# Two-layer pipeline on one Trainium2 core: the planner's order is refined in forward and backward passes, and one-lane loads are paced at 360 GB/s

## The chip, the cores and the metric

The kernel runs on one core of a Trainium2 chip. The metric is the device time in microseconds of one execution, the median of several runs. One further execution was taken with the hardware profiler; every row, wait and clock below comes from that one.

## What is computed

The input is a sequence of 2048 tokens of width 640. Block A is attention with a recurrent memory: the sequence is cut into 64 segments of 32 tokens, and each segment attends, with 32 heads of 192, to itself and to 8 memory rows. The memory rows of a segment's result are the memory of the next segment, so the segments of one layer can only run one after the other. Block B is a token mixer and an MLP with two layer norms and two gelus. Layers A, B, A, B follow each other.

```python
for s in range(n_seg):
    xs = x[:, s * seg_len:(s + 1) * seg_len, :].copy()
    h = jnp.concatenate([mem, xs], axis=1)
    q = jnp.einsum('btd,dhe->bhte', h, Wq)
    ...
    o = jnp.einsum('bhqk,bhke->bhqe', p, v)
    o = jnp.einsum('bhte,hed->btd', o, Wo)
    mem = o[:, :M, :].copy()
    outs.append(o[:, M:, :])
...
x = x + _A_ref(_layernorm(x, axis=-1), ...)
x = x + _B_ref(_layernorm(x, axis=-1), ...)
x = x + _A_ref(_layernorm(x, axis=-1), ...)
x = x + _B_ref(_layernorm(x, axis=-1), ...)
```

## The kernel before, in words

**Steps and lanes.** The kernel runs 69 steps. In step t, lane 0 computes segment t of the first attention layer and lane 1 segment t - 5 of the second, side by side, so that each weight is read once for both. Steps 0 to 4 have only lane 0 and steps 64 to 68 only lane 1; these ten are called one-lane steps here, and steps 5 to 63 two-lane steps. Block B runs in chunks of 64 tokens of each lane, one chunk in every two steps, in between the attention's work.

**Inside a step.** The heads are taken in four pairs of groups. For each pair come the key and query projections (`psk` and `psq`, line 612, functions `fn`), the value projection (`psv`, line 665 with two lanes, 700 with one, `fv`), and for each group of four heads a chain that goes from engine to engine: scores `pss` on TensorE (line 720, `fs`), the row extreme on VectorE (732), the exponential on ScalarE (739), the normalization on VectorE (743 to 745), transposes `pst` on TensorE (754, `f4`), their copy `PT` on ScalarE (762), attention times values `pso` on TensorE (771, `f6`), and its two half copies `oT` (782 on ScalarE, 784 on VectorE). The output projection `psy` (806, `f8`) reads `oT`. At the end of a step the memory rows are copied out of `psy` into the next step's input `hT` (833, `fm`); no projection of the next step can start ahead of that. In block B the pieces of w3 are line 1224 (`psh`), those of w4 line 1269 (`y`), and the gelu's steps lie between lines 894 and 907.

**Weights.** Part of the attention weights stays in SBUF. The rest is streamed by the SP queue into a ring of 12 slots of 384 KB (`RING_A`, tile `wst`, line 490): 23 loads in a step, since the last pair of a step is kept and used first in the next one. Block B's weights go through a ring of three (`wstB`, lines 526 to 532).

**What sets the order.** Nothing is issued where it stands in the source. Every operation is an `Op` with an engine, an estimated duration, a due time written by hand (a place within a step of nominally 48 units) and its dependences. `Plan.place` is a list scheduler on the host: it keeps a time for each engine, for each PSUM and ring slot and for one model of the DMA queues, and of the operations that could start about first on an engine it takes the one with the earliest due time. The resulting list is then emitted; each engine works through its own part of it in that order, and waits where a semaphore says so. The planner's times do not exist on the chip, with one exception: a load that the planner held back for the DMA queues (`paced`) gets a dependence on the last TensorE operation that had ended in the plan when the load was to start. So the load's moment on the chip is a place in TensorE's work. The rate that the planner grants to loads is `DMA_START` in step 0, `RATE_ONE` in the other one-lane steps and `DMA_RATE` in two-lane steps; only step 0's loads are never held back.

```python
s = max(s, srv - ahead(o))
o.paced = s > s0 + 1e-9
...
srv = max(s + DMA_FIRST, srv) + o.dma / (DMA_START if o.due < STEP else RATE_ONE if alone(o) else DMA_RATE)
done = srv + DMA_LAST + o.margin
```

Of the kernel before, what the change touches and what calls it, by code (L numbers as in the profile page):

```python
# [45 lines left out]
ONE = 56  # L46
WARM = (2, 4, 2, 1, 1, 1, 1, 6, 1, 1, 2, 1, 1)
SWITCH = 0.095
LAT = 0.12
PE_LAT = 0.3  # L50
DMA_RATE = 350.0e3
DMA_ISSUE = 0.37
DMA_FIRST = 0.8
DMA_LAST = 3.2
# [2 lines left out]
LEAD_B = 0.0  # L57
DMA_AHEAD = 1.0
DMA_AHEAD_ONE = 1.0
DMA_START = 385.0e3  # L60
RATE_ONE = 400.0e3
NSTEPS = 64
LAST_PACE = 0.55

# [25 lines left out]

class Op:
    __slots__ = ("e", "d", "due", "fn", "n", "succ", "ready", "slots", "start", "end", "dma", "i", "margin",
                 "paced", "last", "after", "mode")


class Plan:
# [8 lines left out]
    def add(self, e, d, due, fn, r=(), w=(), a=(), dma=0, queue=None, margin=0.0, after=(), mode=0, order=()):  # L105
        op = Op()
        op.mode = mode
        op.e, op.d, op.due, op.fn, op.dma, op.margin = e, d, due, fn, dma, margin
        op.succ, op.ready, op.n = [], 0.0, 0
        op.i = len(self.ops)  # L110
        op.paced = False
        op.last = None
        op.after = after
        preds = {*after, *order}
        slots = []
        for b in r:
            preds.update(b.writers)
        for b in w:
            preds.update(b.writers)
            preds.update(b.readers)  # L120
        for b in a:
            preds.update(b.base)
            preds.update(b.readers)
        for b in r:
            b.readers.append(op)
        for b in w:
            b.base = [op]
            b.writers = [op]
            b.readers = []
        for b in a:  # L130
            b.writers.append(op)
        for b in {id(b): b for b in (*r, *w, *a)}.values():
            if isinstance(b, Slotted):
                b.left += 1
                slots.append(b)
        op.slots = slots
        preds.discard(op)
        for p in preds:
            p.succ.append(op)
            op.n += 1  # L140
        self.ops.append(op)
        if queue is not None:
            self.queues.setdefault(queue, []).append(op)
        return op

    def place(self):
        in_queue = {}
        head = {}
        for q, lst in self.queues.items():
            lst.sort(key=lambda o: (o.due, o.i))  # L150
            for k, o in enumerate(lst):
                in_queue[o.i] = (q, k)
            head[q] = 0
        engines = sorted({o.e for o in self.ops})
        cand = {e: [] for e in engines}
        free = dict.fromkeys(engines, 0.0)
        waiting = {}

        def offer(o):
# [12 lines left out]
        mode = 0  # L172
        out = []

        def est(o, t):
            s = max(t, o.ready)
            need = {}
            for b in o.slots:
                if b.slot is None:
                    k, n = need.get(b.cls, (0, 0))  # L180
                    need[b.cls] = max(k, b.keep), n + 1
            for c, (k, n) in need.items():
                fs = self.free_slots[c]
                if len(fs) < n + k:
                    return None
                s = max(s, fs[n - 1][0])
            if o.e == "SP":
                s0 = s
                s = max(s, srv - ahead(o))
                o.paced = s > s0 + 1e-9  # L190
            return s

        def ahead(o):
            if o.due < STEP:
                return 1.0e9
            return DMA_AHEAD_ONE if alone(o) else DMA_AHEAD

        def alone(o):
            return o.due < LAG * STEP or o.due >= NSTEPS * STEP

        while left:
            best = None
            for e in engines:
                t = free[e]
                lst = cand[e]
                if not lst:
                    continue
                vals = []
                m = None
                for o in lst:  # L210
                    s = est(o, t)
                    if s is not None:
                        vals.append((s, o))
                        if m is None or s < m:
                            m = s
                if m is None:
                    continue
                if best is not None and m >= best[0]:
                    continue
                lim = m + (0.12 if e == "PE" else 0.05)  # L220
                stay = e == "PE" and mode
                s, o = min((so for so in vals if so[0] <= lim),
                           key=lambda so: (so[1].mode != mode if stay else False, so[1].due, so[1].i))
                if best is None or s < best[0]:
                    best = (s, o)
            assert best is not None, "no operation can be placed"
            s, o = best
            e = o.e
            for b in o.slots:
                if b.slot is None:  # L230
                    b.slot = self.free_slots[b.cls].pop(0)[1]
# [12 lines left out]
            left -= 1  # L244
            for b in o.slots:
                b.left -= 1
                b.free_at = max(b.free_at, done + LAT)
                if b.left == 0:
                    heapq.heappush(self.free_slots[b.cls], (b.free_at, b.slot))
                    self.free_slots[b.cls].sort()  # L250
            for x in o.succ:
                if o.dma:
                    at = done
                elif x.e == e:
                    at = o.end
                else:
                    at = o.end + (PE_LAT if e == "PE" else LAT)
                if at > x.ready:
                    x.ready = at
                x.n -= 1  # L260
                if x.n == 0:
                    offer(x)
            if o.i in in_queue:
                q, k = in_queue[o.i]
                head[q] = k + 1
                lst = self.queues[q]
                if k + 1 < len(lst) and lst[k + 1].i in waiting:
                    x = waiting.pop(lst[k + 1].i)
                    cand[x.e].append(x)
        return out  # L270
# [3 lines left out]
def kernel(  # L274
# [228 lines left out]
    def load_b(nm, a, e, due, c0=0, c1=None, last=False):  # L503
# [19 lines left out]
        def fn(op):  # L523
# [906 lines left out]
```

## Time and profile before

| what | value |
|---|---|
| median of 3 runs | 3384.89 us (3380.54 to 3385.96) |
| the profiled execution | 3382.05 us, its span 3380.3 us |
| TensorE busy in the span | 3191.1 us, 94% |
| VectorE, ScalarE busy | 2318.0 us, 1908.7 us |
| DMA | 860.40 MB, mean 255 GB/s |
| steps 1 to 4 (one lane), by the trace | 176.0 us, TensorE busy 151.36 us |
| steps 5 to 63 (two lanes) | 2861.7 us, TensorE busy 2775.39 us |
| steps 64 to 67 (one lane) | 184.6 us, TensorE busy 156.53 us |

The steps are cut at the 68 starts of ScalarE's copy of line 833, which ends a step's recurrence: 89.2, 265.2, 3126.9 and 3311.5 us are those after steps 0, 4, 63 and 67. In a row of waits the columns are the instruction, what it waited for, and then the total, the number and the longest. A release called "issue" is idle time for which the profile shows no semaphore.

### The profile page before, as it was taken

How to read it: one execution, taken by the hardware profiler on the slowest of the kernel's cores; microseconds unless marked ns; L12 is line 12 of the kernel's file. 1: busy time of each engine (PE TensorE's matmuls, PEld its weight loads, DVE VectorE, ACT ScalarE, POOL GpSimd, SP SyncE). 2: the span in 40 equal slices, each digit the busy share in tenths (PEclk: the TensorE clock that was granted, in tenths of full speed). 3: DMA queues.
4: the chain of work that ended last, by engine and by line, in shares of the span. 5: the costliest groups of instructions: out<-in, count | busy, mean ns of one | idle time of the engine just before them, and what ended most of it. 6: DMA issues, size and time to landing. Idle time of an engine off the chain costs nothing.

```text
span 3380.3 us, 173603 instructions
## 1 busy us (share of the span) xinstructions
PE 3191.1 (94%) x77341; PEld 2808.9 (83%) x77341; DVE 2318.0 (69%) x6857; ACT 1908.7 (56%) x4837; POOL 237.2 (7%) x485
## 2 busy tenths in 40 slices
PE   6889999999999999999999999999999999999887
PEld 4778888888888888888888888888888888888775
DVE  2665676777677777776767777677777777677665
ACT  2335565656555656565556656555666565556443
POOL 0000000000000000000000000000000000000000
PEclk7999999999999999999999999999999999999999
DMA  9776777778777876787778767877776778777875
GB/s 372 262 271 233 238 270 249 237 240 278 255 244 242 276 250 236 238 277 254 245 233 286 238 231 249 270 250 239 258 268 236 241 260 278 242 240 255 286 249 204
DMA packets 419559, 860.40 MB, mean 255 GB/s; under 512 B 40784, under 2 KB 208415, under 8 KB 418808
## 3 DMA queue, kind: packets, MB, share of 16 engines
q1 hardware_dynamic: 411512, 836.21, 72.2%
q8 instruction: 605, 9.91, 1.2%
q0 software_dynamic: 7136, 13.00, 1.2%
q14 instruction: 146, 1.20, 0.1%
q10 hardware_dynamic: 160, 0.08, 0.0%
HBM read 843.88 MB, written 5.24 MB: 251 GB/s over the span
## 4 chain that ended last, share of the span: by engine, by line
PE 81%; DVE 9%; DMA 4%; ACT 3%; issue 3%; SPq 1%; POOL 0%; DVEq 0%; ACTq 0%
PE psy L806 16%; PE psq L612 16%; PE psk L612 15%; PE psv L665 12%; PE pso L771 4%; PE pss L720 4%; PE y L1269 3%; PE pst L754 3%; PE psh L1224 3%; PE psv L700 2%; DVE oT L784 2%; PE hs L1161 1%; PE psh L1102 1%; ACT oT L782 1%; DMA wstB<-in_B_w_dram 1%
## 5 line engine op out<-in xcount | busy, mean ns | idle before, releaser
L612 PEld LDWEIGHTS <-wst 128*128 128x128 bf16 x19872 | 793.3, 99 | 21.9 <-issue 12.0
L806 PE MATMUL psy<-oT,wo 128*128 128x80 bf16 (+1 forms) x16560 | 685.2, 200 | 69.2 <-DVE oT L784 41.5
L645 ACT CAST V<-psv 96x384 bf16<-96x384 f32 (+3 forms) x1264 | 599.6, 474 | 212.9 <-PE psv L665 123.8
L806 PEld LDWEIGHTS <-wo 128*128 128x128 bf16 x16560 | 628.6, 99 | 81.9 <-issue 71.3
L732 DVE CUSTOM_DVE_ANT_1 pss<-pss,mask 80x320 f32<-80x320 f32 (+2 forms) x552 | 258.9, 469 | 333.9 <-PE pss L720 320.9
L612 PE MATMUL psq<-hT,wst 128*128 128x80 bf16 (+1 forms) x9936 | 474.2, 200 | 11.6 <-issue 7.8
L612 PE MATMUL psk<-hT,wst 128*128 128x80 bf16 (+1 forms) x9936 | 460.1, 200 | 1.5 <-issue 1.0
L665 PEld LDWEIGHTS <-hT 128*32 128x32 bf16 (+1 forms) x11840 | 295.6, 96 | 162.7 <-issue 11.5
L620 ACT CAST qT<-psq 128x480 bf16<-128x480 f32 (+1 forms) x552 | 290.9, 527 | 228.6 <-PE psq L612 224.8
L665 PE MATMUL psv<-wst,hT 128*32 128x384 bf16 x6512 | 367.2, 326 | 1.3 <-DMA wst<-in_A_Wv_dram 0.7
L784 DVE CAST oT<-pso 128x240 bf16<-128x240 f32 (+1 forms) x552 | 214.1, 388 | 224.4 <-ACT oT L782 195.1
L762 ACT COPY PT<-pst 80x320 bf16<-80x320 bf16 (+2 forms) x552 | 222.4, 403 | 214.8 <-PE pst L754 210.5
L612 PE MATMUL psk<-hT,wk 128*128 128x80 bf16 (+1 forms) x6624 | 320.6, 200 | 17.0 <-DVE hT L833 14.9
L612 PE MATMUL psq<-hT,wq 128*128 128x80 bf16 (+1 forms) x6624 | 321.7, 200 | 8.7 <-DMA wq<-in_A_Wq_dram 4.4
L635 ACT CAST kT<-psk 64x160 bf16<-64x160 f32 (+1 forms) x552 | 152.7, 277 | 303.9 <-PE pss L720 171.3
L665 PE MATMUL psv<-wv,hT 128*32 128x384 bf16 x5328 | 321.8, 328 | 0.0
L628 DVE CAST kT<-psk 128x320 bf16<-128x320 f32 (+1 forms) x552 | 255.2, 462 | 92.7 <-ACT kT L635 87.8
L612 PEld LDWEIGHTS <-wk 128*128 128x128 bf16 x6624 | 274.9, 99 | 26.4 <-issue 21.6
L782 ACT CAST oT<-pso 128x240 bf16<-128x240 f32 (+1 forms) x552 | 190.1, 344 | 175.0 <-PE pso L771 137.7
L612 PEld LDWEIGHTS <-wq 128*128 128x128 bf16 x6624 | 267.3, 100 | 10.3 <-issue 5.2
L771 PE MATMUL pso<-PT,V 80*128 80x80 bf16 (+2 forms) x4416 | 244.8, 197 | 23.7 <-ACT PT L762 13.8
L720 PE MATMUL pss<-kT,qT 128*128 128x80 bf16 (+2 forms) x3312 | 243.2, 210 | 9.6 <-issue 4.9
(148 smaller groups left out, 4238.2 us busy)
## 6 DMA issues: line engine op xcount, KB each, us to landing
wst<-in_A_Wk_dram SPq DMA_DIRECT2D x556, 384.0 KB, 5.3
wst<-in_A_Wq_dram SPq DMA_DIRECT2D x556, 384.0 KB, 5.4
wst<-in_A_Wv_dram SPq DMA_DIRECT2D x487, 384.0 KB, 5.4
wstB<-in_B_w_dram SPq DMA_DIRECT2D x495, 320.0 KB, 5.0
wstB<-in_B_w_dram SPq DMA_DIRECT2D x132, 160.0 KB, 4.4
wo<-in_A_Wo_dram SPq DMA_DIRECT2D x8, 960.0 KB, 12.3
xw<-in_A_x_dram POOLq DMA_DIRECT2D x31, 80.0 KB, 4.9
x2d<-vbg POOLq DMA_DIRECT2D x31, 80.0 KB, 5.2
```

What stands on the lines that cost most here:

```text
L612: nc.tensor.matmul(out=o[:, cc, 0:W], lhsT=wv(kc, GW * j + cc * P, GW * j + (cc + 1) * P), rhs=h[:, kc, cw:cw + W], start=(kc == 0 and cc ...
L620: nc.scalar.copy(out=qT[:, :, c0:c0 + N], in_=T(pq)[:, :, off:off + N])
L628: nc.vector.tensor_copy(out=k4[:, :, 0::3, c0:c0 + N], in_=p4[:, :, 0::2, off:off + N])
L645: (nc.vector.tensor_copy if e == "DVE" else nc.scalar.copy)(out=v_part(*dst), in_=a_)
L665: nc.tensor.matmul(out=o[32 * u:32 * u + n3, :], lhsT=left[:, kc, 32 * g3:32 * g3 + n3], rhs=wv(kc, a, a + GWH), start=(kc == 0), stop=(kc ...
L720: nc.tensor.matmul(out=o[0:m_, i * N:(i + w_) * N].rearrange("p (a b) -> p a b", a=w_), lhsT=qTw[:, c * NS:c * NS + m_], rhs=k_[:, j:j + w ...
L732: nc.vector.tensor_tensor_reduce(out=o, in0=o, in1=maskt.unsqueeze(1).to_broadcast([NR, HG, N]), scale=-scale, scalar=3.0e38, op0=ALU.add, ...
L762: nc.scalar.copy(out=Pt[0:KV, :, 0:N], in_=T(pst)[0:KV, :, c0:c0 + N])
L771: nc.tensor.matmul(out=o[:, 3 * hf + c, 0:N], lhsT=V_[0:KV, VP * hf + col:VP * hf + col + P], rhs=Pt[0:KV, 2 * hf + i2, 0:N], start=st, st ...
L782: nc.scalar.copy(out=o_[:, 3:6, off:off + N], in_=T(pso)[:, 3:6, 0:N])
L784: nc.vector.tensor_copy(out=o_[:, 0:3, off:off + N], in_=T(pso)[:, 0:3, 0:N])
L806: nc.tensor.matmul(out=o[:, m, cw:cw + W], lhsT=wo[:, cc, m * P:(m + 1) * P], rhs=o_[:, cc, 0:W], start=st, stop=True, skip_group_check=True)
```

## The change

`place` no longer schedules once. It schedules forward with the due times as priorities, then goes backward through that schedule and gives each operation the latest time at which it may start without moving the end, takes these times as the priorities of the next forward pass, and repeats that five times. The pass whose modelled end is the earliest is then made again and used. The order within the two SP queues still follows the due times. Apart from that two rates of the planner change: loads in step 0 from 385 to 375 GB/s and loads in the other one-lane steps from 400 to 360 GB/s. The operations themselves, their instructions and their data are the same 20,726 as before.

```diff
+PASSES = 5
...
-DMA_START = 385.0e3
-RATE_ONE = 400.0e3
+DMA_START = 375.0e3
+RATE_ONE = 360.0e3
...
+        op.pr = due
...
     def place(self):
+        sizes = {c: len(v) for c, v in self.free_slots.items()}
+        for o in self.ops:
+            o.need = o.n
+        best = None
+        k = 0
+        while k <= PASSES:
+            self.reset(sizes)
+            out = self.forward()
+            end = max(o.end for o in out)
+            if best is None or end < best[0]:
+                best = (end, [o.pr for o in self.ops])
+            k += 1
+            late = self.backward(out, sizes)
+            for o in self.ops:
+                o.pr = late[o.i]
+        for o, p in zip(self.ops, best[1]):
+            o.pr = p
+        self.reset(sizes)
+        return self.forward()
...
+    def backward(self, out, sizes):
+        end = max(o.end for o in out)
...
+        for o in sorted(out, key=lambda o: (-o.start, -o.i)):
+            le = end
+            for x in o.succ:
+                gap = DMA_LAST + o.margin if o.dma else 0.0 if x.e == o.e else PE_LAT if o.e == "PE" else LAT
+                le = min(le, late[x.i] - gap)
+            for b in o.slots:
+                x = follow.get(id(b))
+                if x is not None and x.i in late:
+                    le = min(le, late[x.i] - LAT)
...
+            late[o.i] = le - d
+        return late
+
+    def forward(self):
         in_queue = {}
...
-                           key=lambda so: (so[1].mode != mode if stay else False, so[1].due, so[1].i))
+                           key=lambda so: (so[1].mode != mode if stay else False, so[1].pr, so[1].i))
```

More of the change, by code (lines that the diff above doesn't have):

```diff
@@ L92 @@
     __slots__ = ("e", "d", "due", "fn", "n", "succ", "ready", "slots", "start", "end", "dma", "i", "margin",
-                 "paced", "last", "after", "mode")
+                 "paced", "last", "after", "mode", "pr", "need")
 class Plan:
@@ new lines, in place, with reset @@
+        for o, p in zip(self.ops, best[1]):
+            o.pr = p
+        self.reset(sizes)
+        return self.forward()
+    def reset(self, sizes):
+        self.free_slots = {c: [(0.0, k) for k in range(n)] for c, n in sizes.items()}
+        for o in self.ops:
+            o.n, o.ready, o.paced = o.need, 0.0, False
+            for b in o.slots:
+                b.slot, b.left, b.free_at = None, 0, 0.0
+        for o in self.ops:
+            for b in o.slots:
+                b.left += 1
@@ new lines, in backward @@
+    def backward(self, out, sizes):
+        end = max(o.end for o in out)
+        first, tenants = {}, {}
+        for o in out:
+            for b in o.slots:
+                if id(b) not in first:
+                    first[id(b)] = o
+                    tenants.setdefault((b.cls, b.slot), []).append(b)
+        follow = {id(x): first[id(y)] for lst in tenants.values() for x, y in zip(lst, lst[1:])}
+        late = {}
+        edge = {"PE": end, "SP": end}
+        busy = {}
+        for o in sorted(out, key=lambda o: (-o.start, -o.i)):
[3 more added lines that the diff above has]
+                le = min(le, late[x.i] - gap)
+            for b in o.slots:
+                x = follow.get(id(b))
+                if x is not None and x.i in late:
+                    le = min(le, late[x.i] - LAT)
+            d = o.end - o.start
+            if o.e in edge:
+                le = min(le, edge[o.e])
+                move = o.dma / DMA_RATE
+                edge[o.e] = le - (move if o.dma else d)
+                late[o.i] = le - (max(d, DMA_FIRST + move) if o.dma else d)
+                continue
+            lst = busy.setdefault(o.e, [])
+            k, n = 0, len(lst)
+            while k < n:
+                m = (k + n) // 2
+                if lst[m][0] >= le:
+                    k = m + 1
+                else:
+                    n = m
+            while k < len(lst) and lst[k][1] > le - d:
+                le = min(le, lst[k][0])
+                k += 1
+            lst.insert(k, (le - d, le))
+            late[o.i] = le - d
+        return late
```

## The prediction

> **What bounds the kernel now.** I read the page's first part, then the busy time cut by stage, then the waits of TensorE in each stage, then the timeline at those waits.
>
> ```profile
> PE 3191.1 (94%) x77341; PEld 2808.9 (83%) x77341; DVE 2318.0 (69%) x6857; ACT 1908.7 (56%) x4837; POOL 237.2 (7%) x485
> ```
>
> TensorE bounds it; a new order can only take from the 189.2 us in which TensorE idles, or raise its clock. By stage (length, then busy time by engine, clock, DMA share, GB/s):
>
> ```profile
> 89.20:265.20 176.00, 151.36 (x4014) 128.43 (x4014) 109.45 (x379) 71.89 (x230) 8.48 (x17) 0.95 0.73 256
> 265.20:3126.90 2861.70, 2775.39 (x67201) 2462.84 (x67199) 2034.98 (x5879) 1723.49 (x4249) 204.12 (x411) 1.00 0.74 252
> 3126.90:3311.50 184.60, 156.53 (x4074) 135.89 (x4074) 113.24 (x393) 73.78 (x234) 14.78 (x29) 0.95 0.74 258
> ```
>
> The 59 two-lane steps idle 86.3 us, 1.5 us each. The eight one-lane steps 1 to 4 and 64 to 67 idle 24.6 + 28.1 us, 6.6 us each, at a clock of 0.95. TensorE's waits in the two-lane stage, then in the tail:
>
> ```profile
> PE psy L806 <- DVE oT L784: 36.6, 60, 0.9
> PE psk L612 <- DVE hT L833: 14.9, 29, 0.5
> PE pso L771 <- ACT PT L762: 9.6, 29, 0.3
> PE psq L612 <- issue: 8.7, 15, 1.3
> ```
>
> ```profile
> PE psy L806 <- issue: 11.6, 6, 2.5
> PE psq L612 <- issue: 3.1, 3, 1.9
> ```
>
> In the two-lane stage the waits are few and regular: in the timeline 0.34 us per even step at `pso`, 0.33 (even) and 0.89 (odd) at the step's last `psy`, 0.51 at the odd step's end. In the one-lane steps most idle time is "issue": 15.6 us in the tail (the two rows and 0.9 at `psh`), 13.0 in the head. The timeline of step 65:
>
> ```profile
> 3201.39 0.47 PE L806 MATMUL psy<-oT,wo 128*128 128x56 bf16 x12
> 3204.33 1.03 PE L806 MATMUL psy<-oT,wo 128*128 128x56 bf16 x33 [2.46 <-issue]
> ...
> 3210.55 0.34 PE L700 MATMUL psv<-wv,hT 128*40 128x384 bf16 x2
> ```
>
> ```profile
> 3201.40:3205.40 4.00, 1.54 (x59) 1.43 (x56) 2.04 (x10) 0.39 (x1) 3.09 (x5) 1.00 1.03 380
> 3205.40:3208.80 3.40, 3.40 (x72) 3.40 (x68) 0.45 (x3) 0.87 (x3) 0.00 (x0) 0.50 0.90 283
> ```
>
> TensorE stops between two matmuls of one accumulation, with the DMA engines full at 380 GB/s, and then runs 3.4 us at half clock. The last `psv` starts at 3210.55; its last weights were issued at 3201.4 and took 7.8 us to land, so they had 1.3 us to spare. Landing times (median, last column), two-lane from 265 to 1000 us, then tail:
>
> ```profile
> wst<-in_A_Wv_dram SPq DMA_DIRECT2D x105, 384.0 KB, 5.5
> ```
>
> ```profile
> wst<-in_A_Wv_dram SPq DMA_DIRECT2D x28, 384.0 KB, 6.4
> ```
>
> [...] Step 0, DMA-bound, moved 367, so a plan at 400 promises more than arrives, and one at 360 about what arrives.
>
> **The change part by part.** I compared the two orders operation by operation. All counts are equal. TensorE has 3332 of 8710 operations in another place, at most 23 away; VectorE 1944, ScalarE 1846. POOL swaps block B's result stores with the next chunk's loads (129 of the 130 places that it changes); POOL is busy 7% and its waits are up to 44.9 us long, which hides that; without this cover it would be a 5 us transfer per chunk. SP changes 205 of 2269 places by at most 4, ring loads past one another. Switches of matmul tiling go from 548 to 552, all four in the tail[...].
>
> *Two-lane steps.* The new order repeats: 30 of 132 TensorE operations move in an even step, 63 of 121 in an odd one.
> (1) Even step: a resident key block of 18 matmuls (0.65 us, timeline) goes ahead of the `pso` that waits 0.34 us for PT. Worth the whole row, -9.6 us.
> (2) End of the even step: one w3 block of 10 matmuls (0.53 us) moves ahead of the last `psy`, covering its 0.33 us, and a 5-matmul one (0.27) takes its place under the memory copy. But `pso` now has one `psy` block (0.54) instead of two ahead of it and comes 0.27 us late. From `pso` to the next `psk` is a fixed chain of 3.1 us, so `psk` starts 0.27 late with 0.27 of work done before: 0.
> (3) Odd step: the gelu passes of w3 move from the middle to the start, w3 and w4 blocks earlier, key blocks between the chains. Walking the order with the measured durations I find four waits of 0.13 to 0.24 us for `oT` and none that puts the step's end back: 0, with +0.37 per odd step as the upper bound (the largest shortfall: `psy` 0.51 us nearer to the oT copy with 0.19 spare), +10.7 in all.
> The odd step's 0.89 and 0.51 us stay. Loads keep their lead in TensorE work (mean shift under 0.1 us; one w3 load of an odd step comes 4.8 us later and keeps 0.7). Sum -10, bounds -13 and +5.
>
> *One-lane steps.* Pacing alone moves a load later in TensorE's work.
> (4) In steps 1, 3, 65, 67 and 68 the last `psv` load had 6.1 to 6.6 us of TensorE work between the place that it waits for and its `psv`; now it has 2.2 to 3.8, with landing at 5.1 to 7.8 us. What it had to spare was 2.5, 1.7, 1.3, 1.1 and 0.1 us; with the 2.8, 2.8, 3.9, 4.2 and 2.8 taken away they are short by 0.3, 1.1, 2.6, 3.1 and 2.7, 9.8 us. If landing falls from 6.4 to the two-lane 5.5, three of them win 0.9 back: +7. SP waits in order, so loads behind come later too; even steps keep 0.5 us or more.
> (5) After that `psv`, steps 65 and 3 pass a transpose ahead of the `psy` that waited 0.72 us, which shortens their end by 1.1 and 1.5: -3.
> (6) Issue waits, 28.6 us in eight steps, and half clock, 5% of 360 us. Less backlog should reduce them; but step 1, whose loads landed in 5.0 us, still lost 4.7 us. Bounds: 0 and -28.6 (and below, by the clock); I take a fifth, -6.
> (7) Chains: by their spare time some scores and transposes would wait 1.5 to 3 us more per one-lane step. Most stand just ahead of the late load, under (4), and I count nothing beyond; uncovered they cost up to +19.
> Sum -2, bounds -35 and +25. Step 0's loads are never held back, and two of its TensorE operations move: 0.
>
> Total -12 on 3382.05: 3370. The median shown lies 2.8 us above the profiled execution, so **3373**. A difference of 0.2% (6.8 us) is about what a measurement tells from no change.
>
> **Rivals.**
> (A) Slower: the late loads of (4) come in full, 9.8 us, each stop halving the clock for 3.4 us (1.7 lost, five times: 8.5), plus half of (7), 9.5, with the issue waits unchanged. One-lane +28, less 3 for (5), less 10 two-lane: +15, 3400. It decides from the point where issue waits fall by less than the late loads cost. For it: lead under landing time. Against it: a stop for a load absorbs chain waits. Chance 0.33.
> (B) No change: small waits of the odd step eat (1), and one-lane gains and losses cancel: 3385. For it: every gap is already small. Chance 0.17.
> (C) Issue waits mostly vanish, as in two-lane steps paced at 350, which lose 0.2 us each against 3.6: -10 two-lane, -18 one-lane: 3357. Against it: step 1. It shares the forecast's 0.50.
> That the change does nothing is excluded by the order itself.
>
> **How the numbers follow.** Forecast and C 0.50 faster (forecast alone 3358 to 3378), B 0.17, A 0.33. The range reaches from beyond C, 3350, to a little above A, 3404.
>
> **What would show it.** In the two-lane stage `pso` waiting for PT falls from 9.6 to about 0 and the stage from 2861.7 to about 2852; if `psy` waiting for `oT` grows by as much, (3) failed. In the tail, `psv` at line 700 waiting for Wv appears, 2 to 3 us a step, in 65, 67 and 68; issue falls from 15.6; Wv's landing falls towards 5.5. The forecast is wrong if the two one-lane stages together (360.6 us) grow by more than 8 us, or if the two-lane stage does not shrink.

## The result, and the profile after

The changed kernel takes 3349.41 us (median of 4 runs, 3337.62 to 3354.13), the kernel before on the same chip 3382.72 us (median of 4). The ratio is 0.9896, with a 95% interval of 0.9866 to 0.9926: 1.0% faster. The forecast of 3373 had the sign but a third of the size, and its lowest value, 3350, lies just above the result. The profiled execution of the changed kernel took 3354.13 us, its span is 3352.4 us. Lines of code are 76 higher than before from line 147 on: `psk`, `psq` 688, `psv` 741 (one lane 776), `pss` 796, `pst` 830, `PT` 838, `pso` 847, the halves of `oT` 858 and 860, `psy` 882, the copy to `hT` 909.

The page's first part, the row of busy times:

```profile
PE 3175.4 (95%) x77341; PEld 2808.7 (84%) x77341; DVE 2316.1 (69%) x6857; ACT 1908.5 (57%) x4837; POOL 236.7 (7%) x485
```

TensorE ran the same 77341 matmuls and is called busy for 15.7 us less. No two-lane matmul became shorter: the rows give the same mean durations in both kernels, 202 ns for `psy` and `psq` and 326 for `psv` with streamed weights. A short wait between two groups lies inside the "busy" time that the profile gives the first: of the 0.54 us by which `pso` starts late in the kernel before, from start to start, its row shows 0.34. That matters for all that follows.

The busy time by stage, cut at the same copies as before (columns: stage, length, then PE, PEld, DVE, ACT and POOL, clock, DMA share, GB/s); steps 1 to 4, 5 to 63 and 64 to 67:

```profile
89.40:268.10 178.70, 154.69 (x4035) 132.52 (x4035) 109.92 (x380) 72.12 (x232) 8.26 (x17) 0.94 0.74 253
268.10:3099.40 2831.30, 2755.02 (x67176) 2458.22 (x67176) 2031.69 (x5879) 1723.97 (x4247) 203.97 (x411) 1.00 0.75 254
3099.40:3278.60 179.20, 154.03 (x4074) 131.41 (x4074) 114.20 (x393) 73.02 (x234) 14.61 (x29) 0.97 0.76 265
```

The two-lane stage lost 30.4 us (2861.7 to 2831.3), the two one-lane stages together 2.7 (360.6 to 357.9). Step 0 is the same within 0.2 us, and what follows the last cut took 73.8 us instead of 68.8, at a granted clock of 0.89 instead of 0.94; so the span of the profiled execution fell by 27.9 us. In the two-lane stage 20.4 us of the gain is in TensorE's "busy" (2775.4 to 2755.0) and only 10.0 in its idle time. TensorE's waits there (instruction, what it waited for, total, number, longest):

```profile
PE psy L882 <- DVE oT L860: 27.0, 31, 0.9
PE psk L688 <- DVE hT L909: 21.7, 58, 0.5
PE psq L688 <- issue: 14.8, 24, 1.7
...
PE pso L847 <- ACT PT L838: 0.3, 1, 0.3
```

`pso` waiting for PT is gone (9.6 to 0.3), the 29 waits of `psy` at the end of even steps too (36.6 to 27.0); what is left of `psy` is the 0.9 us of each odd step. `psk` waiting for `hT` has grown by 6.8, all idle "issue" time in this stage from 13.9 to 21.7.

Since idle rows miss the short waits, I measured each place from start to start: from the start of the last matmul of one group to the start of the first of the next, less the usual distance between matmuls of the first group. In one pair of steps (30 and 31), its issue waits left out, in us:

| place | before | after |
|---|---|---|
| even: `pso` behind the PT copy | 0.54 (idle row 0.34) | 0 |
| even: layer norm transposes (line 876, now 952); next `pst` | 0.22; 0.18 (0.05; 0.02) | 0; 0 |
| even, end: last `psy`; `pso` ahead of it; next `psk` | 0.49; 0; 0.12 | 0; 0.21; 0.40 |
| odd: `pst` behind the normalization | 0.32 (0.12) | 0 |
| odd, end: `pso`; the `psy` beside it | 0.19; 0 | 0; 0.16 |
| odd, end: last `psy`; next `psk` | 1.06; 0.68 | 1.06; 0.68 |

The sum is 1.3 us a pair: 0.94 in the even step (its end gains and loses 0.49) and 0.35 in the odd one. The shortest steps agree: the even one fell from 50.40 to 49.67, the odd one from 45.58 to 44.98, 1.33 a pair. (Step 62, the last even one, has another order of work and is left out here and below.) How the 1.33 is split between the two follows the cut and not the waits: the changed kernel does ten `psh` matmuls (0.53 us) ahead of the cut, in the even step, that stood behind it before. Over 29 even and 30 odd steps the falls are 39.2 us; 7.8 of it went into more issue waits, and 31.4 is about the stage's 30.4.

Two of these places in the timeline (start, length, engine, line, operation). First the even step's `pso` in the changed kernel: the key block of 18 matmuls stands ahead of it, and a second one behind it, ahead of `psy`.

```profile
1489.50 0.42 ACT L838 COPY PT<-pst 96x320 bf16<-96x320 bf16 x1
1489.53 0.81 PE L688 MATMUL psk<-hT,wk 128*128 128x80 bf16 x18
...
1490.18 0.46 PE L847 MATMUL pso<-PT,V 96*128 96x80 bf16 x8
...
1490.90 0.81 PE L688 MATMUL psk<-hT,wk 128*128 128x80 bf16 x18
...
1491.54 0.34 PE L882 MATMUL psy<-oT,wo 128*128 128x80 bf16 x5
```

Then the odd step's `pst`, before and after, with VectorE's queue:

```profile
1567.17 0.37 DVE L683 COPY V<-stash 32x896 bf16<-32x896 bf16 x1
...
1567.57 0.48 DVE L743 TENSOR_REDUCE sm<-Pm 80x4 f32<-80x320 bf16 x1
1568.09 0.17 DVE L744 RECIPROCAL sm<-sm 80x4 f32<-80x4 f32 x1
...
1568.30 0.49 DVE L745 TENSOR_TENSOR Pm<-Pm,sm 80x320 bf16<-80x320 bf16 x1
...
1568.84 0.32 PE L754 MATMUL pst<-ident,Pm 80*128 80x80 bf16 x4
```

```profile
1558.28 0.49 DVE L821 TENSOR_TENSOR Pm<-Pm,sm 80x320 bf16<-80x320 bf16 x1
...
1558.80 0.38 DVE L759 COPY V<-stash 32x896 bf16<-32x896 bf16 x1
1558.83 0.32 PE L830 MATMUL pst<-ident,Pm 80*128 80x80 bf16 x4
```

Before, a 0.37 us copy from `stash`, which nobody needs soon, stands ahead of the normalization that `pst` waits for, and `pst` starts 0.54 us after the last normalization instruction starts (0.55 in the changed kernel, where nothing delays it). After, the copy stands behind it. In VectorE's order the same holds for 144 such stash copies (`fst`) and 29 residual adds of block B (`fxu`).

In the one-lane tail (steps 64 to 67), TensorE's waits and the landing of Wv's loads:

```profile
PE psy L882 <- issue: 6.0, 5, 1.8
PE pss L796 <- issue: 4.9, 3, 2.6
PE psq L688 <- issue: 2.4, 2, 2.1
```

```profile
wst<-in_A_Wv_dram SPq DMA_DIRECT2D x28, 384.0 KB, 5.2
```

In step 65 the load for the last `psv` was issued at 3174.11 and landed at 3180.76. TensorE ahead of that `psv`:

```profile
3178.57 0.42 PE L796 MATMUL pss<-kT,qT 128*128 128x40 bf16 x4 [2.55 <-issue]
3179.80 0.47 PE L796 MATMUL pss<-kT,qT 128*128 128x40 bf16 x6 [0.81 <-DVE kT L704]
3180.89 0.45 PE L830 MATMUL pst<-ident,Pm 80*128 80x80 bf16 x4 [0.61 <-DVE Pm L821]
3181.27 0.51 PE L776 MATMUL psv<-wv,hT 128*40 128x384 bf16 x2
```

TensorE stood still for 4.3 us of the 7.2 between that issue and the `psv`, 1.7 of it in the chain of scores and softmax. No `psv` waits for Wv. All issue waits of the tail went from 15.6 to 13.5, those of steps 1 to 4 from 13.0 to 12.0, and Wv lands in 5.2 instead of 6.4 us.

### The profile page after: what moved, and what is told of

Read it like the earlier page. It is cut to its first block, busy times and chain, and to the rows that moved or that the text cites. A ratio compares the mean times of both kernels' runs of the same rounds, so it can differ in the third digit from the quotient of the medians.

```text
span 3352.4 us, 173525 instructions
## 1 busy us (share of the span) xinstructions
PE 3175.4 (95%) x77341; PEld 2808.7 (84%) x77341; DVE 2316.1 (69%) x6857; ACT 1908.5 (57%) x4837; POOL 236.7 (7%) x485
## 4 chain that ended last, share of the span: by engine, by line
PE 89%; DVE 4%; DMA 2%; issue 2%; ACT 2%; SPq 0%; POOL 0%; POOLq 0%; ACTq 0%
PE psk L688 17%; PE psq L688 17%; PE psv L741 15%; PE psy L882 15%; PE pso L847 5%; PE pss L796 4%; PE y L1345 3%; PE psh L1300 3%; PE pst L830 3%; PE psv L776 2%; PE psh L1178 1%; PE hs L1237 1%; DVE oT L860 1%; PE psv L952 1%; DVE sm L819 1%
## 5 line engine op out<-in xcount | busy, mean ns | idle before, releaser
L882 PE MATMUL psy<-oT,wo 128*128 128x80 bf16 (+1 forms) x16560 | 696.2, 200 | 60.8 <-DVE oT L860 31.6
L688 PE MATMUL psk<-hT,wst 128*128 128x80 bf16 (+1 forms) x9936 | 470.3, 200 | 1.7 <-issue 0.9
L688 PE MATMUL psk<-hT,wk 128*128 128x80 bf16 (+1 forms) x6624 | 320.7, 200 | 24.3 <-DVE hT L909 21.7
L688 PEld LDWEIGHTS <-wq 128*128 128x128 bf16 x6624 | 266.3, 100 | 26.5 <-issue 21.7
L796 PE MATMUL pss<-kT,qT 128*128 128x80 bf16 (+2 forms) x3312 | 243.2, 209 | 13.9 <-DVE kT L704 7.5
```

What stands on the lines that cost most here:

```text
L688: nc.tensor.matmul(out=o[:, cc, 0:W], lhsT=wv(kc, GW * j + cc * P, GW * j + (cc + 1) * P), rhs=h[:, kc, cw:cw + W], start=(kc == 0 and cc ...
L796: nc.tensor.matmul(out=o[0:m_, i * N:(i + w_) * N].rearrange("p (a b) -> p a b", a=w_), lhsT=qTw[:, c * NS:c * NS + m_], rhs=k_[:, j:j + w ...
L882: nc.tensor.matmul(out=o[:, m, cw:cw + W], lhsT=wo[:, cc, m * P:(m + 1) * P], rhs=o_[:, cc, 0:W], start=st, stop=True, skip_group_check=True)
```

## The experiments

Ratios are against the kernel before on the same chip, with 95% intervals. The two-lane stage and the shortest steps come from one profiled execution of each kernel, cut at the copies to `hT`, as above. The stage varies between executions: 2831.3, 2834.7 and 2837.0 us for three kernels with the changed kernel's two-lane order (the change, with old rates, with `oT` split), whose shortest steps agree within 0.01 us. So the shortest steps tell more than the stage. Because of the ten matmuls, those of a kernel that starts from before are to be compared with before, and the others with the change. Where a kernel starts from before, the edit works on the planner's finished list: an operation is moved only past operations that it does not depend on.

| kernel | median us | ratio | two-lane stage | shortest even, odd |
|---|---|---|---|---|
| before | 3382.72 | 1 | 2861.7 | 50.40, 45.58 |
| the change | 3349.41 | 0.9896 (0.9866 to 0.9926) | 2831.3 | 49.67, 44.98 |
| change with old rates | 3349.96 | 0.9909 (0.9890 to 0.9928) | 2834.7 | 49.68, 44.98 |
| before with new rates | 3382.21 | 0.9996 (0.9984 to 1.0008) | 2863.1 | 50.39, 45.57 |
| before, key block moved | 3386.12 | 1.0017 (1.0005 to 1.0029) | 2866.0 | 50.57, 45.57 |
| before, copies behind | 3384.66 | 1.0009 (0.9999 to 1.0020) | 2876.4 | 50.66, 45.28 |
| before, both | 3386.31 | 1.0018 (1.0004 to 1.0033) | 2870.7 | 50.82, 45.28 |
| before, key block, banks exchanged | 3384.01 | 1.0000 (0.9985 to 1.0014) | 2858.8 | 50.40, 45.58 |
| before, copies behind, VectorE's half first | 3370.18 | 0.9970 (0.9953 to 0.9987) | 2852.5 | 50.16, 45.28 |
| before, these three | 3366.14 | 0.9945 (0.9927 to 0.9964) | 2850.6 | 50.16, 45.28 |
| before, and second key block | 3367.02 | 0.9960 (0.9945 to 0.9974) | 2851.5 | 50.11, 45.27 |
| before, whole row of key blocks | 3384.18 | 0.9995 (0.9984 to 1.0007) | 2862.6 | 50.70, 45.28 |
| change, key block back | 3360.49 | 0.9937 (0.9913 to 0.9961) | 2842.5 | 50.11, 44.98 |
| change, copies back | 3383.30 | 1.0010 (0.9996 to 1.0024) | 2871.6 | 50.23, 45.52 |
| change, `oT` split | 3346.94 | 0.9905 (0.9882 to 0.9927) | 2837.0 | 49.68, 44.98 |
| change, and one `hT` copy | 3343.86 | 0.9879 (0.9854 to 0.9904) | 2821.4 | 49.47, 44.78 |
| change, and half first | 3333.96 | 0.9852 (0.9833 to 0.9870) | 2811.7 | 49.48, 44.39 |

### Order or rates

```diff
-DMA_START = 375.0e3
-RATE_ONE = 360.0e3
+DMA_START = 385.0e3
+RATE_ONE = 400.0e3
```

The changed kernel with the old rates:

> The changed kernel with the two rates put back (385 and 400 GB/s): only the passes are left. Theory (the order of the two-lane steps is the gain): the two-lane stage stays near 2831 us and the whole lies within 6 us of the changed kernel, ratio 0.988 to 0.992. Rival (the rates carry part of it): the whole is 8 to 15 us slower than the changed kernel, ratio 0.993 or more, with the loss in the one-lane steps and landing of the tail's Wv back at 6 us and more.

The kernel before with the new rates:

> The kernel before with only the two load rates of the change (375 and 360 GB/s in the plan instead of 385 and 400). Theory (the rates are nearly nothing either way, since the changed kernel with the old rates ran at 0.9909): two-lane stage 2862 as before, one-lane stages within 3 us of before with the last Wv loads landing with under 1 us to spare, total 3378 to 3388 (0.999 to 1.002). Rival (my forecast's own step on late loads): `psv` waits for Wv in steps 65, 67 and 68, total up by 7 us, 1.002 or more.

The old rates leave 0.9909, within the interval of the change; the new ones alone bring 0.9996. The gain is the order's, and the rates are nothing that these runs can tell. No `psv` of the tail waits for Wv with the new rates alone either.

### The named parts, each on the kernel before

```diff
+    for x, o, y in zip(pe, pe[1:], pe[2:]):      # scores, pso, key block
+        if (...) == (715, 766, "fn") and y.d > 0.5 and (...):
+            moved["key"] += earlier(placed, y, o)
```

> The kernel before with one thing done: in 28 even two-lane steps the resident key block of 18 matmuls is put ahead of the pso that waits for PT. Theory (a wait is worth the whole delay of the matmul's start, 0.54 us of which the profile shows 0.34 as idle): two-lane stage -15 us, 28 times 0.54. Rival (the idle row is the price, as in the prediction's step 1): -9.6 us. Third (the wait only moves on to the next psy, which waits for oT): 0.

```diff
+    for k, o in enumerate(dve):
+        if o.fn.__name__ not in ("fst", "fxu") or not LAG * STEP <= o.due < NSTEPS * STEP:
+            continue
+        for x in dve[k + 1:k + 6]:
+            if x.fn.__code__.co_firstlineno == 742 and x.start - o.start < 1.8:
+                moved["copy"] += later(placed, o, x)
+                break
```

> The kernel before with one thing done: on VectorE, in the two-lane steps, each stash copy and each residual add that stands shortly ahead of a softmax normalization goes behind it (173 moved). Theory (these short operations delay the normalization and the layer norm that TensorE waits for: 0.32 us at an odd step's pst, 0.22 at psn and 0.18 at a pst in the even step): -0.72 us per pair of steps, -21 us. Rival (the prediction's: VectorE's order changes nothing that TensorE waits for): 0, within 3 us.

Both together:

> The kernel before with both single edits (key block ahead of pso, short copies behind the normalization). Theory: they add, -15 and -21, two-lane stage about -36 us, a pair of undisturbed steps at 94.7 us as in the changed kernel. Rival: the changed kernel needs the whole reordering, and these two give less than 15 us together.

None of them brought anything. The key block alone took the wait over, and the even step became 0.17 us longer. TensorE's waits in the two-lane stage:

```profile
PE psk L612 <- ACT PT L762: 9.1, 28, 0.3
```

The planner had given that key block the PSUM bank of `pst`, which comes free only when the PT copy has read it: the very copy that `pso` waits for. In the changed kernel the same block has another bank, which a V copy frees. The copies alone shortened the odd step by 0.30 us, which is the 0.32 of `pst` in the table above, and made the even step 0.26 us longer. There the layer norm transposes and the next `pst` still came 0.23 and 0.19 us late, from start to start, since VectorE stood still until ScalarE had made its half of `oT`:

```profile
1522.84 0.41 DVE L784 CAST oT<-pso 128x240 bf16<-128x240 f32 x1 [0.84 <-ACT oT L782]
```

Before, two of the short operations stand in that time. Behind the normalization they delay a `kT` copy, for which `pss` now stops for 0.20 us. The stage of 2876.4 us is no measure of this edit: its profiled execution was the second slowest of 22, with 22.8 us of issue waits (13.9 before).

### The parts with what they need

```diff
+            if earlier(placed, y, o):
+                moved["key"] += 1
+                swap_banks(placed, y, o)
```

> The kernel before, with the 28 key blocks of the even two-lane steps placed ahead of `pso`, as when they were moved alone (that run: 1.0017 of before, with the wait for PT standing at the key block instead of `pso`), and from there on the PSUM banks of `psk` and `pso` exchanged, so that the key block no longer writes the bank that the PT copy has to empty. Theory (the bank kept the wait alive): the wait for PT is gone from both places, the shortest even step falls from 50.40 to about 49.86 us (0.54 us from start to start), the two-lane stage by up to 28 x 0.54 = 15 us, the total to about 3370 (0.996 of before). Rival 1 (only the idle row counts): 28 x 0.34 = 9.6 us, 3374. Rival 2 (what is saved here is lost at the end of the step or in issue waits): 3381 to 3386, 1.000 to 1.002.

```diff
+    for o, d in zip(dve, dve[1:]):               # residual add, VectorE's half of oT
+        if o.fn.__name__ == "fxu" and d.fn.__code__.co_firstlineno == 780 and (...):
+            a = next(...)                        # ScalarE's half of the same oT
+            moved["half"] += earlier(placed, d, a)
```

> The kernel before, with the 173 stash copies and residual adds placed behind the softmax normalization and layer norm, as when they were moved alone (1.0009 of before; only the odd step gained 0.30 us), and with VectorE's half of the `oT` copy placed ahead of ScalarE's half in the 29 places where it stood behind. Theory (the two halves run one after the other in the order in which they are placed, and ScalarE's half waits behind an exp, so the VectorE queue stood still for 0.84 us): the shortest even step falls from 50.40 to about 50.0 us, the odd one to 45.28 or less, the two-lane stage by about 29 x (0.40 + 0.30) = 20 us, the total to about 3361 (0.994). Rival (the order of the halves is nothing): even step 50.40, total 3381 to 3385, as with the moved copies alone.

All three:

> All three edits on the kernel before: key blocks with exchanged banks, copies behind, VectorE's half first. Theory (these three are the two-lane gain of the change): the shortest pair of steps falls from 95.98 us to about 94.7 (94.66 in the changed kernel), the two-lane stage from 2861.7 to about 2830, the total to about 3349 (0.990 to 0.991). Rival (the gains overlap at the end of the step, where TensorE waits for `oT` and the key block whatever comes before): less than half, 3366 or more (0.9955 or more), and the rest of the change's gain comes from orders not named yet.

With the bank exchanged `pso` no longer waits, and neither does the key block: of the rows for PT one wait of 0.2 us is left. But the even step stays at 50.40 and the total at 1.0000, since the next link took the wait, here `psy`, in 28 more places than before (36.6 us, 60 waits):

```profile
PE psy L806 <- DVE oT L784: 45.8, 88, 0.9
```

`psy` follows `pso` and needs its `oT` copy; the key block had stood between the two and now stands ahead of both. VectorE's half first, with the copies behind, is a gain of 0.3%, about half of what I expected: the odd step is 0.30 us shorter, the even one 0.24 (0.50 against the copies alone), and the delays at the layer norm and the next `pst` are gone. The three together reach 0.9945, half of the change's gain, with the same shortest steps; `psy` has 85 waits, as with the key block's bank exchanged alone (88). So my theory that these three are the change fell; the rival "less than half" came nearest.

### Following the wait along the chain

```diff
+                p = next(...)   # psy behind pso
+                q = next(...)   # the key block behind that psy
+                moved["second"] += earlier(placed, q, p)
```

> The kernel before with the three edits of the last run of this kind (0.9945), and a fourth: the second key block, which stood behind the `psy` that follows `pso`, is placed ahead of that `psy` too, as in the changed kernel. In the last run the wait for PT at `pso` was gone, but the same `psy` then waited 0.35 us (0.52 from start to start) for the DVE half of `oT`. Theory (each step of the chain PT, pso, oT, psy needs its own cover, and the first block alone only moves the wait by one link): that delay goes, the shortest even step falls from 50.16 to about 49.65 us (49.67 in the changed kernel), the two-lane stage from 2850.6 to about 2836, the total to about 3351 (0.990 to 0.991 of before). Rival (the end of the even step takes it): even step stays at 50.1 or more, total 3364 or more (0.9945).

```diff
+                moved["third"] += earlier(placed, b[0], r)      # ahead of the next group's pst
+                moved["fourth"] += earlier(placed, b[a], u) and earlier(placed, b[a + 1], u)   # ahead of its pso
```

> The kernel before with the four edits of the last run (0.996) and two more in each of the 28 even steps: the third key block ahead of the transposes `pst` of the next group (which in the last run waited 0.27 us for the softmax weights), and the two key blocks after it ahead of the `pso` that follows; TensorE's order there is now that of the changed kernel. Theory (the whole row of key blocks has to move by one place; each block moved alone hands the wait to the next link of the chain): the shortest even step falls from 49.95 to about 49.68 us, the odd one stays at 45.27, the two-lane stage falls by 28 x 0.27 = 8 us to about 2843, the total to about 3357 (0.992 to 0.993 of before). Rival (the end of the step or issue waits take it): even step 49.95, total 3364 or more (0.9945 or more).

The second block took away `psy`'s 28 waits (back to 36.5 us, 60), and the next link, `pst`, waited for its softmax weights instead:

```profile
PE pst L754 <- DVE Pm_e L745: 4.7, 18, 0.3
```

That is 0.44 us from start to start, so the even step fell from 50.16 to 50.11 instead of 49.65, and the total, 0.9960, is no better than without it. With the whole row moved, which gives TensorE the changed kernel's order in that stretch, the even step rose to 50.70 and the gain was lost again (0.9995): one of the moved blocks, a query block of 18 matmuls, now waits for a bank. Waits of the stage, and the place in the timeline, whose last row shows only the six of these matmuls that started within the window:

```profile
PE psq L612 <- DVE kT L635: 10.6, 21, 0.6
```

```profile
1506.56 0.69 DVE L683 COPY stash<-V 32x896 bf16<-32x896 bf16 x2
...
1507.28 0.42 DVE L898 SCALAR_TENSOR_TENSOR vbg<-vbg,psh 128x256 f32<-128x256 f32 x1
1507.73 0.33 DVE L635 CAST kT<-psk 64x160 bf16<-64x160 f32 x1
...
1508.11 0.38 PE L612 MATMUL psq<-hT,wq 128*128 128x80 bf16 x6 [0.57 <-DVE kT L635]
```

Its bank is that of the first moved block, and it comes free when VectorE has made the last `kT` copy, which stands behind a normalization, two stash copies and a gelu pass. In the changed kernel that copy is the second of `kT`'s in a row, ahead of all of these, and the query block has another bank. TensorE's order, PSUM's banks and VectorE's order hang together here; the key blocks, copied one by one, handed the wait on (1.0000, 0.9960 and 0.9995).

### The parts taken out of the changed kernel

```diff
+        if (...) == (791, "fn", 842) and y.d > 0.5 and (...):    # scores, key block, pso
+            moved += earlier(placed, o, y)
```

> The changed kernel with one part undone: in its 29 even two-lane steps `pso` stands ahead of the 18-matmul key block again, all else as the change has it. Theory (with the later blocks already moved, this cover is worth what it measures where it stands): `pso` waits 0.34 us for PT again at 29 places (0.54 from start to start), the shortest even step rises from 49.67 to about 50.2 us, the two-lane stage by 29 x 0.54 = 15.7 us to 2847, total about 3364 (0.994 to 0.995 of before). Rival 1 (my forecast's price, the idle row): 29 x 0.33 = 9.6 us, 3359. Rival 2 (later waits have slack enough, as when this part alone on the kernel before brought nothing): 3349 to 3352, 0.990 to 0.991.

```diff
+    for o, x in (...):          # the 173 pairs: stash copy or residual add, normalization
+        moved += earlier(placed, ix[o], ix[x])
```

> The changed kernel with one part undone: the 144 stash copies and 29 residual adds stand ahead of the softmax normalization (and so of the layer norm) on VectorE again, all else as the change has it. Theory (VectorE's short work that nobody waits for delayed work that TensorE waits for): the transposes `pst` of the odd step wait 0.3 us again and `psn` or `pst` of the even step up to 0.4, two-lane stage up by 9 to 20 us, total 3358 to 3369 (0.993 to 0.996 of before). Rival (TensorE's new order leaves enough between, so that the place of these copies no longer matters): 3349 to 3352, 0.990 to 0.991.

Here the parts have a size. The key block back behind `pso` costs 11 us (3360.49 against 3349.41). The intervals of the two ratios overlap, so this rests on the shortest even step too, which rose by 0.44, 12.8 us in 29 places: the theory's 15.7 was high, the idle row's 9.6 low. Its waits:

```profile
PE pso L847 <- ACT PT L838: 8.1, 29, 0.3
```

That is 0.28 us a piece as idle time, 0.48 from start to start, 13.8 us in 29 places. The copies put back ahead cost 34 us (3383.30), as much as the whole change brought. TensorE's waits in the two-lane stage, and the odd step's `pst` in the timeline:

```profile
PE pst L830 <- DVE Pm_e L821: 10.7, 28, 0.7
PE pst L830 <- DVE Pm L821: 9.7, 26, 0.4
```

```profile
1573.53 0.39 DVE L759 COPY V<-stash 32x896 bf16<-32x896 bf16 x1
...
1573.95 0.48 DVE L819 TENSOR_REDUCE sm<-Pm 80x4 f32<-80x320 bf16 x1
...
1575.22 0.32 PE L830 MATMUL pst<-ident,Pm 80*128 80x80 bf16 x4 [0.38 <-DVE Pm L821]
```

From start to start these are 0.54 us in the even and 0.58 in the odd step, 29 x 1.12 = 32 us: the loss. The idle rows show 20.4 of it. This is more than what these places cost in the kernel before, 0.40 and 0.32 us, 21 us in all. So 34 us is what the copies cost in the changed order, and not what moving them brought. The two parts do not add up to the gain, since each is measured with the other in place.

### A version that beats both

What the change leaves is the 0.89 us of each odd step, where the chain ends in two half copies of `oT` that never overlap, and the two copies to `hT`.

```diff
-    oT = [ctile([P, GC, NS], bf16, f"oT{i}") for i in range(OT_BUFS)]
+    oT = [[ctile([P, GC // 2, NS], bf16, f"oT{i}{s_}") for s_ in "ab"] for i in range(OT_BUFS)]
```

> The changed kernel with each `oT` buffer made of two tiles, one for each half, the order of all work unchanged. Theory (the two half copies run one after the other only because both write one tile): at the end of the odd step VectorE's half starts with ScalarE's instead of 0.39 us later, `psy` there waits 0.5 us instead of 0.89, the shortest odd step falls from 44.98 to about 44.6 us, the two-lane stage by some 29 x 0.39 = 11 us to 2820, total about 3338 (0.987 of before). Rival (they take turns for another reason, such as the PSUM bank of `pso` that both read): nothing, odd step 44.98, total as the changed kernel, 3349.

```diff
+        if len(take) == 2:
+            def fm2(op):
+                src = T(psy)[:, :, SEG:SEG + 2 * M].rearrange("p k (l m) -> p k l m", l=2)[:, :, ::-1, :]
+                nc.scalar.copy(out=hn[:, :, SEG:SEG + 2 * M].rearrange("p k (l m) -> p k l m", l=2), in_=src)
```

> As with the split `oT` buffers, and the two copies of 8 memory columns that end a two-lane step (ScalarE for one lane, then VectorE for the other, into one hT tile, 0.19 and 0.20 us one after the other) made one ScalarE copy that writes both, so that the next key block waits for one copy. Theory: the wait of `psk` for hT falls from 0.51 to about 0.3 us in odd steps and by up to as much in even ones, 58 x 0.2 = 12 us off the two-lane stage on top of the split, total about 3327 (0.984 of before). Rival (a longer strided copy costs what two cost, or the wait is then for the yTB copy or an issue): within 3 us of the kernel with the split alone.

```diff
+    for a, d in zip(two, two[1:]):               # the last two halves of oT in a step
+        if (a.e, d.e) == ("ACT", "DVE") and a.slots[0] is d.slots[0]:
+                ...
+                placed.remove(d)
+                placed.insert(x, d)
```

> As the kernel with one hT copy (0.9879 of before), and at the end of each two-lane step VectorE's half of the `oT` copy placed ahead of ScalarE's: the program makes the two take turns at the `pso` tile that both read, and the first `psy` after it needs VectorE's half only. Theory: at the end of the odd step `psy` waits 0.5 us instead of 0.89 (ScalarE's half is then under the 15 matmuls of that first `psy`, 0.54 us), 29 x 0.39 = 11 us less, total about 3333 (0.985 of before). Rival (the second `psy` then waits as long for ScalarE's half): less than 3 us, 3341 to 3344.

Splitting `oT` did nothing. In the timeline of that kernel the halves, now in two tiles, still follow one another:

```profile
1559.88 0.36 ACT L858 CAST oT0b<-pso 128x240 bf16<-128x240 f32 x1 [0.54 <-PE pso L847]
1560.27 0.41 DVE L860 CAST oT0a<-pso 128x240 bf16<-128x240 f32 x1 [1.50 <-ACT oT0b L858]
1560.73 0.70 PE L883 MATMUL psy<-oT0a,wo 128*128 128x80 bf16 x15 [0.89 <-DVE oT0a L860]
```

By the program's semaphores VectorE is released by ScalarE's half, although the two share only the tile that they read, `pso`. Since the first `psy` needs VectorE's half alone, it is enough to place that one first. The last kernel, at the same place:

```profile
1555.60 0.41 DVE L860 CAST oT0a<-pso 128x240 bf16<-128x240 f32 x1 [1.44 <-PE pso L847]
1556.05 0.36 ACT L858 CAST oT0b<-pso 128x240 bf16<-128x240 f32 x1 [0.98 <-DVE oT0a L860]
1556.07 0.70 PE L883 MATMUL psy<-oT0a,wo 128*128 128x80 bf16 x15 [0.50 <-DVE oT0a L860]
...
1557.34 0.23 ACT L909 CAST hT<-psy 128x80 bf16<-128x80 f32 x1 [0.93 <-PE psy L883]
```

`psy` waits 0.50 instead of 0.89, and ScalarE's half lies under its first 15 matmuls: 9.9 us by the medians, against 11 expected, and 0.39 us off the shortest odd step (the intervals overlap slightly). The single `hT` copy takes 0.23 us in place of 0.19 and 0.20 one after the other. The waits of `psk` for it fell from 21.7 to 9.1 us, the shortest steps by 0.2 us each and the stage by 15.6, but the median by only 3.1 (intervals overlap), so its own worth stays open. With all of it the kernel takes 3333.96 us, 0.9852 of before; this interval and that of the change touch as well.

## Why the prediction was wrong

**The step that failed is (3), the odd step, put at 0, and with it the even step, which had no term at all for the same cause.** I walked TensorE's order with the measured durations and took the other engines' work as arriving when it had arrived before. I had counted that VectorE has 1944 operations in another place and never costed them. In the kernel before, VectorE's order held TensorE up by 0.32 us at the odd step's `pst` and by 0.40 us at the even step's layer norm transposes and the `pst` behind them, from start to start: 21 us in 59 steps, more than half of what the places of the table add up to. The change took all of it. On the kernel before, the copies placed behind took the 0.32 away; the 0.40 went only when VectorE's half of `oT` came first as well. The 0.60 us by which the shortest odd step fell is not the measure of (3): 0.53 is the ten matmuls on the other side of the cut, 0.35 the waits, and the `psk` behind the cut lost 0.28.

**Term (1)**, the key block, had the right mechanism and the wrong size. I priced it by its idle row, 9.6 us; its start-to-start delay was 0.54 and not 0.34 us, 15.7 us in 29 places, and undone in the changed kernel it costs 11 us. On its own it was worth nothing: it needs another PSUM bank, and the links behind it need cover too.

**Term (2)** held: at the end of the even step `psy` lost 0.49, `pso` and `psk` gained 0.21 and 0.28.

**Terms (4) to (7).** The one-lane sum of -2 met -2.7 by cancellation. The late loads of (4) cost at most 0.1 us instead of 7. The five landed with 1.0, 0.0, 0.5, -0.1 and 1.0 us to spare, and not short by up to 3.1. One reason is that those of steps 65, 67 and 3 landed in 6.7, 4.3 and 4.9 us (7.8, 6.8 and 7.5 before), where I had let the landing fall by 0.9. The other is the chain waits of (7), of 1.1 to 1.8 us, which stand just ahead of that `psv`, where (7) had placed them. The 367 GB/s of step 0, from which I argued about the rates, are a mean and no limit in the trace: slices of 2.2 us in it moved up to 406, and the stretch of step 65's stop 380. Issue waits (6) fell by 3.1 instead of 6; that less backlog reduces them was an estimate of mine and is not shown. One pair of executions says little here: the two stages took 354.4 to 364.9 us in the nine traces with the one-lane steps of before (358.6 on average), 346.5 to 357.9 in the six with the order and the rates of the change (351.9), so about -7; the last stretch was 2.8 us longer in these six. With the new rates alone the two stages took 360.1 us.

**The sum and the range.** Two-lane was to be -10 with bounds of -13 and +5, and measured -30.4: 15.7 at `pso`, 21 by VectorE's order and 1 at the odd step's end, less the 7.8 of more issue waits. The prediction shows no working for its -13, which lies near the one idle row that it took; but the stage's idle time fell by only 10.0, and 20.4 us of the gain was in time that the page calls busy. "A new order can only take from the 189.2 us in which TensorE idles" was the sentence that misled me.

**Rivals.** A (late loads cost in full) and B (no change) did not happen. The half clock that A counts for each stop was an estimate from one stop of step 65, of 2.46 us, followed by 3.4 us at a granted clock of 0.50; another of that step, of 2.36 us, left the clock at 1.00. C came near in time, 3357, with the wrong place: -18 from one-lane issue waits, where the gain was two-lane.

What stays open: the parts that I named reproduce half of the gain on the kernel before. The rest is in how banks, VectorE's and TensorE's orders fit, shown for single places, not added up. VectorE's half first without the copies behind was not run. Why the issue waits of the two-lane stage differ between these executions, from 13.2 to 26.5 us, was not tried; the most came with the copies put back, in one of the longest stages.

## What to carry to other kernels

Price a reordering on every engine's queue, above all on short work that nobody waits for standing ahead of work that TensorE waits for (34 us here with the copies put back), and ask of each moved block whose buffer it now needs (28 waits of up to 0.3 us for PT, at the key block moved alone). Here one block moved alone handed the wait to the next link (28 more waits of `psy`, ratio 1.0000, for the key block with its bank exchanged); to size a part, take it out of the version in which all the others stand. Measure waits from start to start, not by idle rows (0.54 against 0.34 us at `pso`).

## What the runs showed that I had not expected

Part of each of TensorE's waits, about 0.2 us at the places compared here, did not show as idle time: 0.54 from start to start showed as 0.34, 0.58 as 0.38, 0.22 as 0.05, and TensorE was "busy" 20.4 us less in the two-lane stage with all but 25 of its 67,201 matmuls. In this program two engines that read one PSUM tile, `pso`, took turns, 0.36 and then 0.41 us, also when they wrote to different tiles; whether two PSUM tiles would let them overlap was not tried. One strided copy of 128x80 took 0.23 us where two of 128x40 took 0.19 and 0.20.
